# One decode layer, forward and backward: w_o in rows of 8 KB, and zero fills moved to earlier stages

## The chip, the cores and the metric

The kernel runs on one core of a Trainium2 chip. The metric is the time of one execution on the device in microseconds; of several runs the median is taken. A profile is one further execution with the hardware profiler on.

## The reference, cut to what matters

One token passes an adaptive-LayerNorm block: attention of 32 query heads (4 key/value heads, head size 128) over the last 4096 positions of a cache of 65536, then a gated feed-forward network. The program returns the output and, for a given `grad_out`, the gradient of every input.

```python
q = (x @ wq) ...; k, v = k_cache[:, :, Sk - W:, :], v_cache[:, :, Sk - W:, :]   # W = 4096 of Sk = 65536
p = softmax(q k^T * Dh**-0.5);  o = p v;  attn = o.reshape(B, Sq, Hq * Dh) @ wo  # wo: 4096 x 1024
...
mod = (silu(c) @ w_mod).reshape(c.shape[0], 6, 1, -1)          # w_mod: 1024 x 6144
h = layernorm(x) * (1 + ca) + sa;  x = x + ga * A(h)
h = layernorm(x) * (1 + cb) + sb;  x = x + gb * B(h)            # B: (sigmoid(h w_gate) * (h w_up)) w_down, F = 3584
...
_out, _vjp = jax.vjp(_f, A_x, A_k_cache, A_v_cache, A_wq, A_wo, B_w_gate, B_w_up, B_w_down, c, w_mod)
```

With one token almost every gradient of a weight is the outer product of two vectors, as large as the weight. The gradients of the two caches are zero outside the last 4096 positions, so most of what is written is zeros: 120 pieces of about 1 MB, called fills below.

## The kernel before, in words

Everything is laid out by hand in one SBUF buffer, `arena`, of 192 KB in each of 128 partitions; `ar(off, size)` is a slice of it, in KB. The order of instructions on every engine is the order in which the Python code issues them. Five stages follow one another.

1. **Load** (to about 75 us): keys, wq and values are loaded, q, scores and the softmax are made.
2. **N** (75 to 155 us): for each of the 4 key/value heads 32 steps of two matmuls (line 716) on products that VectorE makes (L236). The result `N_sb` holds for every query head a 128x128 matrix. A unit `t_unit(h)` multiplies the stored blocks of wq, `a4[:, j, h, :]`, by that matrix: two matmuls of 128x128 by 512 columns (L674), each evicted at once into the block that it read (L676, or L245 on VectorE). The units of head groups 0 to 2 are put as side jobs at every odd step of this loop; those of group 3 (`tlast`) come at the start of the next stage.
3. **B** (155 to 310 us): 64 chunks (`bch`, L773) of 8 matmuls on TensorE multiply these blocks by w_o. Between them lie the attention output (`attn_units`, L799), the modulation weights, and their transposes.
4. **FFN** (310 to 433 us): seven blocks q of w_up, w_gate and w_down. `front(q)` makes the products with w_up and w_gate on TensorE. `turn(q)` then does the gates; transposes three of eight tiles (`turned`, L1053); multiplies the four rows of w_down on VectorE (`wd_ttr`, L253) and on TensorE (`ffn_mm`, L1073); starts the next load of w_down (`load_wd`, L931, in two halves, from SyncE's queue) as the rows become free; issues fills; and makes the row `dug_b`. Two transposes of side jobs are put between (`side(2)`). VectorE then does the other five tiles and the loads of w_up and w_gate for block q+2 are issued (L942).
5. **End** (433 to 600 us): outer products on VectorE (L249) make the weight gradients, which are stored from there: `dwd` (w_down), `dw_rows` (w_up, w_gate; L1107), `dwo` (w_o; L1247), `sec` (w_mod; L1242), `dwq_tile` (wq; L1290), and the cache gradients (L1286).

**w_o.** `load_wo(u)` (L385) brings 512 rows of w_o into `wo_t[u]`. Before, partition d holds the rows 128 a + d for a = 0..3: one row of 2 KB for each of four heads. The gradient is stored with another order: partition p holds the four rows 4p..4p+3, which are 8 KB in one piece. For it the vector o is put in that order by `op_ps` (L1196, 16 small fp32 matmuls) at the beginning of the End stage.

**Queues.** GpSimd (POOL) issues all fills, most loads and most stores, in the order of the code. SyncE (SP) issues the loads of w_down, a few of w_mod, and some of the last stores.

**Fills.** `zero(n)` issues the next n of the 120 fills. The lists `Z_...` at the top say how many are issued at each place, and `zero(len(zleft))` at the very end issues what is left. A fill can wait for an instruction (`after`), which keeps it from being issued earlier than that. In N and B the pieces are copied from a zeroed piece in DRAM (L203); elsewhere they come from a small tile of zeros (L209; six of them in a narrow form, L194 and L197).

**Buffers of the row gradients.** `dw_rows(k, j, off, ...)` writes a tile of 7 KB a partition at arena offset `off` and stores it. In the End stage three offsets, 16, 32 and 40, go round; VectorE has to wait until the store from a buffer has landed before it writes there again.

Of the kernel before, what the change touches and what calls it, by code (L numbers as in the profile page):

```python
# [10 lines left out]
P = 128  # L11
# [13 lines left out]
HQ = 32  # L25
# [26 lines left out]
Z_KC = [0] * 8  # L52
Z_SM = 4
Z_N = spread(31, 128)
Z_B = [n + (i in (31, 38)) for i, n in enumerate(spread(29, 43))] + [1, 1, 1, 1, 0] + [1, 0, 0, 1, 1, 1, 0, 0] + [1, 0, 1, 0, 1, 0, 0, 0]
Z_FOLD = (1, 1, 1, 2)
Z_FFN = [(1, 0, 1)] + [(1, 1, 1)] * 4 + [(0, 2)]
Z_HAND = (1, 1, 2, 1, 1)
Z_ROWS = (1, 1, 1, 0, 1, 0, 1, 0)
JT = 3  # L60
JV = KD - JT
@with_exitstack
def kernel(
# [314 lines left out]
    def wo_dram(t, u):  # L378
        return t[u * 512:(u + 1) * 512, :].rearrange("(a d) n -> d a n", d=DH)

    def dwo_dram(u):
        return out_5[u * 512:(u + 1) * 512, :].rearrange("(p a) n -> p a n", a=4)

# [263 lines left out]
    def ok_rows():  # L647
        cp(o_col, ok_ps[:, 0:HQ])
        cp(kb_col, ok_ps[:, HQ:2 * HQ])
        cp(o_bf, o_col)  # L650
        lo = scr[:, 768:832].bitcast(FP32)
        for k, (col, rows, s) in enumerate(((o_col, o_rows, 1.0), (kb_col, nkb_rows, -1.0))):
            st = st_cols[k].rearrange("p (a h) -> p a h", a=4)
            cp(st[:, 0, :], col)
            tt(lo, col, st[:, 0, :], ALU.subtract)
            cp(st[:, 3, :], lo)
            cp(st[:, 1, :], st[:, 3 - 3 * k, :])
            cp(st[:, 2, :], st[:, 3 * k, :])
# [46 lines left out]
    for g in range(G):  # L705
        nbank = bank_pair("n_ps", g)
        for t_ in range(KT):
# [35 lines left out]
    tlast = [t_unit(h, "AV") for h in range(HG * 3, HQ)]  # L743


# [38 lines left out]
    for i in range(4):  # L784
        bch()
        tlast[2 * i]()
        tlast[2 * i + 1]()
    bch(2)
# [5 lines left out]
    def attn_units(us, first):  # L794
        for a in range(4):
            for k in range(2):
                for c in range(4):
                    h = 4 * us[c] + a
                    nc.tensor.matmul(attn4[k][32 * c:32 * c + 32, :], lhsT=o_bf[:, h:h + 1].broadcast_to([P, 32]),  # L799
                                     rhs=wo_t[us[c]][:, a, k * 512:(k + 1) * 512], start=(first and a == 0),  # L800
                                     stop=(not first and a == 3), tile_position=(0, 32 * c))
# [245 lines left out]

    def turned(q):
        for j in range(JT):
# [142 lines left out]
    dln2 = vt([P, KD], "dln2")  # L1192
    op_ps = new_acc("op_ps")
    for hh in range(4):
        for a in range(4):
            nc.tensor.matmul(op_ps[32 * hh:32 * hh + 32, 8 * a:8 * a + 8], lhsT=ident_f[:, a::4], rhs=o_col[:, hh::4],  # L1196
                             start=True, stop=True, tile_position=(0, 32 * hh))
    o_perm = kb_col
    cp(o_perm, op_ps[:, 0:HQ])
    mulv(dln2, dh2, cb1)  # L1200
# [26 lines left out]
    dmod_b2 = ar(160, 4)  # L1227
    sec_t = [ar(o, 8) for o in (0, 8, 152, 32, 40, 16, 48, 56)]
    dv_home, dk_home = [ar(o, 32).rearrange("p (g x) -> p g x", g=G) for o in (64, 96)]
# [14 lines left out]
    def dwo(u):  # L1244
        for a in range(4):
            outer_dve(wo_t[u][:, a, :], o_perm[:, 8 * a + u:8 * a + u + 1], dattn_b)
        nc.gpsimd.dma_start(out=dwo_dram(u), in_=wo_t[u])  # L1247

# [96 lines left out]
    bcast(dmod_bf[:, 16:48], 32, dmod_b4, "A")  # L1345
    dw_rows(1, 0, 40, outer_dve)
    zero(Z_ROWS[4])
    dw_rows(1, 1, 16, outer_dve)
    dwo(1)
# [7 lines left out]
    pd = b1k.bitcast(FP32)[:, 0:HQ]  # L1357
    dw_rows(1, 2, 32, outer_dve)
    zero(Z_ROWS[5])
    dw_rows(1, 3, 40, outer_dve)  # L1360
    dcs234 = matvec_T(lambda jb, nb: w2_t[jb][:, nb * P:(nb + 1) * P], dh2_hl, "dcs234")
# [9 lines left out]
    sec(0)  # L1371
    dw_rows(1, 4, 16, outer_dve)
    zero(Z_ROWS[6])
    sec(1)
    dw_rows(1, 5, 32, outer_dve)
    for run in vT_unit[12:]:
        run()
    rebuild_P()
    bcast(dq_bf, HQ, dq_b, "A")
    dw_rows(1, 6, 40, outer_dve)  # L1380
    zero(Z_ROWS[7])
    dw_rows(1, 7, 16, outer_dve)
    sec(2)
# [113 lines left out]
```

## Time and profile before

| | |
|---|---|
| runs | 602.09, 599.39, 599.31 us; median 599.39 |
| the profiled execution | 602.02 us, of which the span from the first to the last instruction is 600.2 us |
| busy in the span | TensorE 415.4 us, VectorE 353.8, ScalarE 247.5, GpSimd 148.0 |
| DMA | 246.54 MB in 33645 packets, mean 411 GB/s |
| HBM | 78.13 MB read, 185.60 MB written |
| fills | 46 from the tile of zeros, 68 from DRAM, 6 in the narrow form |
| loads of w_o | 8 of 1024 KB, median 12.5 us from issue to landing |

The span is counted from the first instruction, and all times below are on that clock. The profiled execution's own time is 1.8 us above its span. The page cuts the span into 40 slices; its row "DMA" tells in tenths how busy the 16 DMA engines were, and the row "GB/s" what they moved. Shares of a queue can add up to over 100%, since packets overlap.

### The profile page before, as it was taken

Reading aid. Unit: us, or ns where it says so; the run is one execution under the profiler, and the core shown is the slowest. Engines: PE = TensorE matmul, PEld = TensorE weight load, DVE = VectorE, ACT = ScalarE, POOL = GpSimd, SP = SyncE. Lnnn points to the kernel's source line nnn. Section 1 sums busy time; section 2 is a strip of 40 time slices with the busy share of each in tenths; the row PEclk is TensorE's granted clock in tenths of the full one; section 3 lists DMA queues with packets and bytes.
Section 4 is the critical chain, followed back from the end, with each engine's and each line's share of the span. In section 5 each row is a group of like instructions: output and inputs, shape, how many; then the busy total and the mean of one; then the engine's idle time right before and its main releaser. Section 6 shows DMA issues by size and latency. Waiting matters only on the chain.

```text
span 600.2 us, 9825 instructions
## 1 busy us (share of the span) xinstructions
PE 415.4 (69%) x4004; PEld 246.7 (41%) x4004; DVE 353.8 (59%) x647; ACT 247.5 (41%) x398; POOL 148.0 (25%) x249
## 2 busy tenths in 40 slices
PE   3996789999999999979776477766652056364300
PEld 2784434334345455435455465555532045131000
DVE  3755499999510030194738488878877056876800
ACT  2489515558211024112246366665632057373200
POOL 3113113212222122222223033241335133241100
PEclk9998699999999999998988578787676557555555
DMA  8999999999999999999999999999999999999997
GB/s 349 421 418 423 411 457 406 430 424 438 433 420 391 453 433 393 461 425 412 387 417 417 347 355 408 409 409 421 424 425 425 429 396 425 423 425 419 419 415 235
DMA packets 33645, 246.54 MB, mean 411 GB/s; under 512 B 4781, under 2 KB 4781, under 8 KB 18864
## 3 DMA queue, kind: packets, MB, share of 16 engines
q0 software_dynamic: 28320, 225.98, 93.8%
q1 hardware_dynamic: 5232, 19.93, 9.5%
q8 instruction: 31, 0.51, 0.3%
q14 instruction: 14, 0.11, 0.1%
q10 hardware_dynamic: 48, 0.01, 0.0%
HBM read 78.13 MB, written 185.60 MB: 439 GB/s over the span
## 4 chain that ended last, share of the span: by engine, by line
PE 37%; DMA 21%; DVE 20%; ACT 8%; issue 7%; POOL 3%; ACTq 0%; POOLq 0%; DVEq 0%; SPq 0%
PE b_ps L773 17%; DMA out_dram<-arena 12%; DVE arena L236 6%; PE n_ps L716 6%; DMA arena<-in_B_w_down_dram 5%; DVE arena L249 4%; DVE arena L253 3%; ACT arena L527 2%; ACT arena L1281 2%; PE t_ps L674 2%; DMA out_dram<-zeros 2%; DVE scr L253 2%; DMA arena<-in_B_w_gate_dram 1%; PE tp_k L506 1%; PE tp_side L916 1%
## 5 line engine op out<-in xcount | busy, mean ns | idle before, releaser
L773 PE MATMUL b_ps<-arena 128*128 128x512 bf16 x512 | 118.6, 384 | 1.1 <-ACT arena L917 1.1
L917 ACT COPY arena<-tp_side 128x1024 bf16<-128x1024 bf16 x62 | 60.8, 1018 | 50.5 <-PE tp_side L916 50.3
L236 DVE TENSOR_TENSOR arena<-arena 128x2048 bf16<-128x2048 bf16 x64 | 76.5, 1223 | 2.3 <-PE n_ps L716 0.3
L773 PEld LDWEIGHTS <-arena 128*128 128x128 bf16 x512 | 49.3, 99 | 58.9 <-issue 5.8
L716 PE MATMUL n_ps<-arena 128*128 128x512 bf16 x256 | 65.6, 378 | 5.8 <-DVE arena L236 4.2
L203 POOL DMA_DIRECT2D out_dram<-out_dram x68 | 33.7, 496 | 116.8 <-PE n_ps L716 38.4
L916 PE MATMUL tp_side<-ident_bf,arena 128*128 128x128 bf16 x496 | 48.2, 262 | 12.7 <-DVE arena L236 4.7
L916 PEld LDWEIGHTS <-arena 128*128 128x128 bf16 x496 | 40.3, 120 | 22.1 <-issue 13.6
L249 DVE TENSOR_SCALAR arena<-arena,h 128x3584 bf16<-128x3584 bf16 (+1 forms) x24 | 28.6, 1192 | 32.1 <-DMA out_dram<-arena 32.1
L209 POOL DMA_DIRECT2D out_dram<-zeros x46 | 25.9, 566 | 67.6 <-DVE rows_all L236 23.0
L716 PEld LDWEIGHTS <-arena 128*128 128x128 bf16 x256 | 24.6, 97 | 41.2 <-issue 15.8
L253 DVE CUSTOM_DVE_ANT_0 arena<-arena,scr 128x1024 bf16<-128x1024 bf16 x35 | 40.8, 1220 | 0.2
L1277 PE MATMUL ps_kv<-arena 32*128 32x512 bf16 x64 | 24.2, 588 | 22.6 <-DVE arena L257 12.8
L253 DVE CUSTOM_DVE_ANT_0 scr<-arena,b1k 128x1024 bf16<-128x1024 bf16 x28 | 34.2, 1223 | 7.5 <-DMA arena<-in_B_w_down_dram 7.0
L1281 ACT ACTIVATE arena<-ps_kv 128x512 bf16<-128x512 f32 x48 | 25.4, 690 | 31.3 <-PE ps_kv L1277 31.1
L676 ACT CAST arena<-t_ps 128x512 bf16<-128x512 f32 x56 | 30.1, 589 | 12.1 <-PE t_ps L674 12.1
L245 DVE CAST arena<-b_ps 128x512 bf16<-128x512 f32 x6 | 4.2, 692 | 50.8 <-PE b_ps L773 50.8
L1053 PE MATMUL tp_ug<-ident_bf,arena 128*128 128x128 bf16 x168 | 14.4, 244 | 17.7 <-ACT arena L1054 17.7
L527 ACT COPY arena<-tp_wq 128x1024 bf16<-128x1024 bf16 x23 | 21.4, 1066 | 7.3 <-PE tp_wq L525 7.3
L1277 PEld LDWEIGHTS <-arena 32*128 32x128 bf16 x64 | 6.9, 117 | 38.7 <-issue 37.8
L1341 PE MATMUL dh_ps<-dattn_bf,arena 128*128 128x1 bf16 x48 | 2.1, 167 | 29.2 <-ACT arena L1337 29.2
L942 POOL DMA_DIRECT2D arena<-in_B_w_up_dram x14 | 10.7, 761 | 43.1 <-DVE dh2acc L253 22.7
(325 smaller groups left out, 686.8 us busy)
## 6 DMA issues: line engine op xcount, KB each, us to landing
out_dram<-zeros POOLq DMA_DIRECT2D x46, 1024.0 KB, 11.8
out_dram<-arena POOLq DMA_DIRECT2D x35, 1024.0 KB, 11.8
out_dram<-arena POOLq DMA_DIRECT2D x16, 896.0 KB, 11.5
arena<-in_A_wq_dram POOLq DMA_DIRECT2D x8, 1024.0 KB, 21.1
arena<-in_A_wo_dram POOLq DMA_DIRECT2D x8, 1024.0 KB, 12.5
arena<-in_w_mod_dram POOLq DMA_DIRECT2D x7, 1024.0 KB, 18.7
arena<-in_B_w_up_dram POOLq DMA_DIRECT2D x14, 512.0 KB, 9.4
arena<-in_B_w_gate_dram POOLq DMA_DIRECT2D x14, 512.0 KB, 13.3
```

Of the source, the lines that this page charges most:

```text
L203: ins = nc.gpsimd.dma_start(out=as_rows(region, BIGP).bitcast(FP32), in_=zero_src[:, 0:P * ZW // 4].rearrange("i (p x) -> (i p) x", p=BIGP ...
L236: return nc.vector.tensor_tensor(out=out, in0=a, in1=b, op=op)
L249: return nc.vector.tensor_scalar(out=out, in0=a, scalar1=s1, scalar2=None, op0=op0)
L253: return nc.vector.tensor_tensor_reduce(out=out, in0=w, in1=b, scale=1.0, scalar=0.0, op0=ALU.mult, op1=ALU.add, accum_out=acc)
L527: nc.scalar.copy(out=blk, in_=tp[:, :])
L676: nc.scalar.copy(out=o, in_=ps)
L716: mm = nc.tensor.matmul(nbank[k][:, :], lhsT=k_nat[:, g, t_ * DH:(t_ + 1) * DH], rhs=vp[:, t_ % 2, 4 * k:4 * k + 4, :].rearrange("p h d -> ...
L773: mm = nc.tensor.matmul(bbank[p][k][:, :], lhsT=a4[:, p, h, :], rhs=wo_t[u][:, a, k * 512:(k + 1) * 512], start=(i == 0 and a == 0), stop= ...
L916: nc.tensor.transpose(tp[:, i * P:(i + 1) * P], blk[:, i * P:(i + 1) * P], ident_bf[:, :])
L917: nc.scalar.copy(out=blk if dst is None else dst, in_=tp[:, :])
L1277: nc.tensor.matmul(ps[:, :], lhsT=rows[r, t8 * P:(t8 + 1) * P], rhs=bd[r, :], start=True, stop=True, tile_position=(32 * tc_, 0))
L1281: nc.scalar.activation(out=o, in_=v, func=ACT.Copy, scale=float(scale))
```

## The change

- **w_o order.** `load_wo` uses the order of the store, `(p a) n -> p a n`: four neighbouring rows, 8 KB, in each partition. What meets w_o has to follow. The T units are rewritten: `t_unit(u, k, a)` takes every fourth column of `N_sb` for four heads and makes four matmuls of 32 output rows each, in the four column tiles of TensorE, into one bank; after a = 3 all four banks are evicted (same number and size of evictions, 64 units of four matmuls instead of 64 matmuls). A fourth bank (`acc`) is used. One unit is put at a side place, 16 a head group instead of 8. o is put in the same order (`shuffle_o`, the code of `op_ps` moved from the End stage to step 6 of the N loop), and the eviction of do puts its columns in that order.
- **turn.** Two of three tiles are transposed first; then the w_down work; the third tile and one side job come after the products `ffn_mm`; the other side job comes after `turned_mm`. The fills of a turn are issued after that side job's instructions.
- **Buffers.** The row gradients use seven offsets: 16, 32, 40 and also 64, 72, 80, 88, where the last four tiles of w_o were.
- **Fills.** One more in `Z_SM` (before the N loop), three more in `Z_N`, two more in `Z_FOLD` (around `front(0)` and `turn(0)`); three fewer in `Z_ROWS` (End). What `zero(len(zleft))` issues at the very end follows from the sum of the lists: 117 of 120 were listed before, 120 are listed now, so three are left over before and none now. Counted in this way six fills leave the End stage.

The diff, cut to its core:

```diff
-Z_SM = 4
-Z_N = spread(31, 128)
+Z_SM = 5
+Z_N = spread(34, 128)
...
-Z_FOLD = (1, 1, 1, 2)
+Z_FOLD = (1, 1, 2, 3)
...
-Z_ROWS = (1, 1, 1, 0, 1, 0, 1, 0)
+Z_ROWS = (1, 1, 0, 0, 0, 0, 0, 0)
...
     def wo_dram(t, u):
-        return t[u * 512:(u + 1) * 512, :].rearrange("(a d) n -> d a n", d=DH)
-
-    def dwo_dram(u):
-        return out_5[u * 512:(u + 1) * 512, :].rearrange("(p a) n -> p a n", a=4)
+        return t[u * 512:(u + 1) * 512, :].rearrange("(p a) n -> p a n", a=4)
...
-        cp(o_bf, o_col)
...
+    o_perm = kb_col
+
+    def shuffle_o():
+        op_ps = new_acc("op_ps")
+        for hh in range(4):
+            for a in range(4):
+                nc.tensor.matmul(op_ps[32 * hh:32 * hh + 32, 8 * a:8 * a + 8], lhsT=ident_f[:, a::4], rhs=o_col[:, hh::4],
+                                 start=True, stop=True, tile_position=(0, 32 * hh))
+        cp(o_perm, op_ps[:, 0:HQ])
+        cp(o_bf, o_perm)
...
-    def t_unit(h, engs="AA"):
+    t_pools = ((psum, "mm"), (pgu, "gu"), (px, "x"), (pacc, "acc"))
+    t_banks = []
+
+    def t_unit(u, k, a, engs="AAAA"):
         def run():
-            for k in range(2):
-                j1 = min(4 * k + 4, NT)
-                ps = new_ps("t_ps").rearrange("p (j m) -> p j m", j=4)[:, 0:j1 - 4 * k, :]
-                o = a4[:, 4 * k:j1, h, :]
-                nc.tensor.matmul(ps, lhsT=N_sb[:, h * P:(h + 1) * P], rhs=o, start=True, stop=True)
-                if engs[k] == "A":
-                    nc.scalar.copy(out=o, in_=ps)
+            pl, tag = t_pools[a]
+            ps = pl.tile([P, 512], FP32, name="t_ps", tag=tag)
+            t_banks.append(ps)
+            for hh in range(4):
+                h = 4 * u + hh
+                nc.tensor.matmul(ps[32 * hh:32 * hh + 32, :].rearrange("p (j m) -> p j m", j=4),
+                                 lhsT=N_sb[:, h * P + a:(h + 1) * P - 3 + a:4], rhs=a4[:, 4 * k:4 * k + 4, h, :],
+                                 start=True, stop=True, tile_position=(0, 32 * hh))
+            if a < 3:
+                return
+            for i in range(4):
+                o, v = a4[:, 4 * k:4 * k + 4, 4 * u + i, :], t_banks[i].rearrange("p (j m) -> p j m", j=4)
+                if engs[i] == "A":
+                    nc.scalar.copy(out=o, in_=v)
                 else:
-                    cp(o, ps)
+                    cp(o, v)
+            t_banks.clear()
         return run
...
+            elif s == 6:
+                shuffle_o()
...
-            jobs.extend(t_unit(h, "AA") for h in range(HG * g, HG * g + HG))
+            jobs.extend(t_units(g))
...
     def turn(q, fills=0):
         gates()
-        turned(q)
-        side(2)
+        turned(q, range(JT - 1))
         wd_ttr(0)
         hh_ops(q)
         first = wd_ttr(1)
         ffn_mm(q, 0)
         if q + 1 < NB:
             load_wd(q + 1, 0, 2)
+        ffn_mm(q, 2)
+        turned(q, (JT - 1,))
+        side(1)
         zero(fills, wd_ttr(2, 3))
-        ffn_mm(q, 2)
         if q + 1 < NB:
             load_wd(q + 1, 2, 2)
         last = dug_part(q)
         turned_mm(q)
+        side(1)
         return first, last
...
-        nc.scalar.copy(out=do_sb, in_=do4[:, :])
+        nc.scalar.copy(out=do_sb.rearrange("q (h r a) -> q a h r", h=4, a=4),
+                       in_=do4.rearrange("q (a h r) -> q a h r", a=4, h=4))
...
-    dw_rows(0, 5, 40, outer_dve)
-    dw_rows(0, 6, 16, outer_dve)
+    dw_rows(0, 5, 64, outer_dve)
+    dw_rows(0, 6, 72, outer_dve)
     zero(Z_ROWS[3])
-    dw_rows(0, 7, 32, outer_dve)
+    dw_rows(0, 7, 80, outer_dve)
...
-    dw_rows(1, 0, 40, outer_dve)
+    dw_rows(1, 0, 88, outer_dve)
...
```

The later calls of `dw_rows` and the list `sec_t` take their offsets in the new round; `attn_units` reads o in the new order, `dwo` stores through `wo_dram`.

More of the change, by code (lines that the diff above doesn't have):

```diff
@@ L666, in build_bd, with t_units @@
                                  scale=sel[:, HG * g + i:HG * g + i + 1])
-    def t_unit(h, engs="AA"):
+    t_pools = ((psum, "mm"), (pgu, "gu"), (px, "x"), (pacc, "acc"))
+    t_banks = []
+    def t_unit(u, k, a, engs="AAAA"):
         def run():
-            for k in range(2):
-                j1 = min(4 * k + 4, NT)
-                ps = new_ps("t_ps").rearrange("p (j m) -> p j m", j=4)[:, 0:j1 - 4 * k, :]
-                o = a4[:, 4 * k:j1, h, :]
-                nc.tensor.matmul(ps, lhsT=N_sb[:, h * P:(h + 1) * P], rhs=o, start=True, stop=True)
-                if engs[k] == "A":
-                    nc.scalar.copy(out=o, in_=ps)
-                else:
-                    cp(o, ps)
-        return run
+            pl, tag = t_pools[a]
[12 more added lines that the diff above has]
+                    nc.scalar.copy(out=o, in_=v)
+                else:
+                    cp(o, v)
+            t_banks.clear()
+        return run
+    def t_units(g, engs="AAAA"):
+        return [t_unit(u, k, a, engs) for u in (2 * g, 2 * g + 1) for k in range(2) for a in range(4)]
     jobs.clear()
@@ L739 @@
         if g < 3:
-            jobs.extend(t_unit(h, "AA") for h in range(HG * g, HG * g + HG))
+            jobs.extend(t_units(g))
     load_wo(3)
     side(len(jobs))
-    tlast = [t_unit(h, "AV") for h in range(HG * 3, HQ)]
+    tlast = t_units(3, "AVAV")
     bq = []
@@ L785 @@
         bch()
-        tlast[2 * i]()
-        tlast[2 * i + 1]()
+        for run in tlast[4 * i:4 * i + 4]:
+            run()
     bch(2)
@@ L797, in attn_units @@
                 for c in range(4):
-                    h = 4 * us[c] + a
-                    nc.tensor.matmul(attn4[k][32 * c:32 * c + 32, :], lhsT=o_bf[:, h:h + 1].broadcast_to([P, 32]),
+                    n = 8 * a + us[c]
+                    nc.tensor.matmul(attn4[k][32 * c:32 * c + 32, :], lhsT=o_bf[:, n:n + 1].broadcast_to([P, 32]),
                                      rhs=wo_t[us[c]][:, a, k * 512:(k + 1) * 512], start=(first and a == 0),
@@ L1046, in ug_flat, with turned @@
         return ug_v[:, q % 2, j // 4, j % 4, :, :].rearrange("p k f -> p (k f)")
-    def turned(q):
-        for j in range(JT):
+    def turned(q, js=range(JT)):
+        for j in js:
             w, tp = ug_flat(q, j), new_tp("tp_ug")
@@ L1192 @@
     dln2 = vt([P, KD], "dln2")
[L1193 to L1199, printed above, removed]
     mulv(dln2, dh2, cb1)
@@ L1227 @@
     dmod_b2 = ar(160, 4)
-    sec_t = [ar(o, 8) for o in (0, 8, 152, 32, 40, 16, 48, 56)]
+    sec_t = [ar(o, 8) for o in (0, 8, 152, 16, 32, 40, 48, 56)]
     dv_home, dk_home = [ar(o, 32).rearrange("p (g x) -> p g x", g=G) for o in (64, 96)]
@@ L1246, in dwo @@
             outer_dve(wo_t[u][:, a, :], o_perm[:, 8 * a + u:8 * a + u + 1], dattn_b)
-        nc.gpsimd.dma_start(out=dwo_dram(u), in_=wo_t[u])
+        nc.gpsimd.dma_start(out=wo_dram(out_5, u), in_=wo_t[u])
     def rebuild_P():
@@ L1345 @@
     bcast(dmod_bf[:, 16:48], 32, dmod_b4, "A")
-    dw_rows(1, 0, 40, outer_dve)
+    dw_rows(1, 0, 88, outer_dve)
     zero(Z_ROWS[4])
-    dw_rows(1, 1, 16, outer_dve)
+    dw_rows(1, 1, 40, outer_dve)
     dwo(1)
@@ L1357 @@
     pd = b1k.bitcast(FP32)[:, 0:HQ]
-    dw_rows(1, 2, 32, outer_dve)
+    dw_rows(1, 2, 16, outer_dve)
     zero(Z_ROWS[5])
-    dw_rows(1, 3, 40, outer_dve)
+    dw_rows(1, 3, 32, outer_dve)
     dcs234 = matvec_T(lambda jb, nb: w2_t[jb][:, nb * P:(nb + 1) * P], dh2_hl, "dcs234")
@@ L1371 @@
     sec(0)
-    dw_rows(1, 4, 16, outer_dve)
+    dw_rows(1, 4, 40, outer_dve)
     zero(Z_ROWS[6])
     sec(1)
-    dw_rows(1, 5, 32, outer_dve)
+    dw_rows(1, 5, 16, outer_dve)
     for run in vT_unit[12:]:
@@ L1379 @@
     bcast(dq_bf, HQ, dq_b, "A")
-    dw_rows(1, 6, 40, outer_dve)
+    dw_rows(1, 6, 32, outer_dve)
     zero(Z_ROWS[7])
-    dw_rows(1, 7, 16, outer_dve)
+    dw_rows(1, 7, 40, outer_dve)
     sec(2)
```

## The prediction

> **What bounds the kernel now.** I read the page's slices first, then busy time by stage, then who waited in the stages where the transfers dip, then single issues in the timeline. The slices show transfers without a break:
>
> ```profile
> DMA  8999999999999999999999999999999999999997
> GB/s 349 421 418 423 411 457 406 430 424 438 433 420 391 453 433 393 461 425 412 387 417 417 347 355 408 409 409 421 424 425 425 429 396 425 423 425 419 419 415 235
> ```
>
> No compute engine is above 69% (PE 415.4 us). So the time is the bytes (246.54 MB) at the rate of a full stretch, 411 to 430 GB/s, plus the time in which no transfer was waiting. Moving a fill saves nothing in itself; it pays where it fills a hole. Slices 22 and 23 (347, 355) are a hole, and by stage (columns: window, length, busy time and count of PE, PEld, DVE, ACT, POOL, then clock, DMA share, GB/s):
>
> ```profile
> 310.00:335.00 25.00, 16.77 (x256) 13.05 (x256) 15.86 (x34) 16.89 (x23) 5.17 (x8) 0.81 1.07 402
> 335.00:350.00 15.00, 8.82 (x144) 6.80 (x144) 10.98 (x24) 4.49 (x5) 2.71 (x5) 0.64 0.90 303
> 350.00:433.00 83.00, 56.73 (x836) 46.76 (x835) 71.96 (x153) 54.11 (x71) 24.69 (x40) 0.74 1.12 411
> 433.00:485.00 52.00, 15.47 (x230) 11.19 (x230) 26.00 (x68) 11.95 (x14) 15.48 (x22) 0.63 1.05 426
> 485.00:490.00 5.00, 4.23 (x69) 4.15 (x70) 1.72 (x2) 3.39 (x7) 1.23 (x2) 0.50 0.86 358
> 490.00:569.00 79.00, 41.03 (x363) 20.97 (x361) 60.68 (x109) 37.38 (x69) 21.10 (x32) 0.54 1.02 421
> ```
>
> Two holes: 335 to 350 lacks (411 - 303) x 15 us = 1.62 MB, 3.9 us of full rate; 485 to 490 lacks (424 - 358) x 5 = 0.33 MB, 0.8 us. The first one's cause, from the waits in 312 to 350 (total, times, longest):
>
> ```profile
> POOL out_dram L209 <- DVE rows_all L236: 11.6, 1, 11.6
> ...
> DVE scr L253 <- DMA arena<-in_B_w_down_dram: 7.0, 2, 4.9
> ```
>
> GpSimd issues nothing from 329.8 to 341.35: its next fill waits for the last w_down row of turn(1), and that half of w_down, issued at 319.94, is there only at 338.5. The second one's cause, from the waits of VectorE in 430 to 570:
>
> ```profile
> DVE arena L249 <- DMA out_dram<-arena: 38.4, 11, 13.9
> ```
>
> The outer products wait 38.4 us for stores from their own buffers (13.9 of it at 475.6, for offset 16), and the queue runs dry at 488.
>
> **The change part by part.** One fill is 1.049 MB; in the trace fills land 2.41 to 2.45 us apart.
>
> *Four fills earlier in softmax and N.* No hole lies there (80 us at 432 GB/s), so they only push what is queued behind them back by 4 x 2.43 = 9.7 us. GpSimd issues at most eight transfers ahead (in B each lands 19 us after issue, 8 x 2.42), the rest of the push is blocked issue. Who waits: w_o(3), landing at 174.1 and used at about 175.7, so chunk 10 of B comes some 8 us late; the ga weights (landed 210.77, used at 210.72); the last modulation load (landed 305.84, its product starts 306.23). B is gated by such loads anyway, so FFN starts about 9.7 us later, with the same transfers queued behind it as before: no transfer time is lost, and TensorE gains 9.7 us of cover up to there.
>
> *T in column tiles.* 256 matmuls for 64. The price is shown by the attention products, 128x32 by 512 in four column tiles:
>
> ```profile
> L799 PE MATMUL attn<-arena,o_bf x64: 379/379/390, 179.2 to 191.3; 128*32 128x512 bf16 x64
> ```
>
> The chain of waits has 32 of them in 1.84 us, 0.23 for four, against 1.73/8 = 0.216 for one full matmul. 64 x 0.014 = +0.9 us, and up to 64 x 0.3 more if four weight loads (97 ns each) don't hide. With one unit at each of 48 side places, where 0.43 us were taken at each of 24, the N loop (VectorE's 1.23 of 1.29 us a pair of steps) keeps its pace. shuffle_o adds its 1.47 us of PE there. Under the 9.7 us cover: 0; beyond it each us costs one only once the eight transfers ahead are used up.
>
> *w_o in 8 KB rows.* The eight loads land 2.53 to 2.70 us after the transfer before them (one 3.95, with other traffic), about 2.55; the wq loads, 8 KB rows, 2.48 apart. 8 x 0.07 = 0.5 us less. Bounds: 0, and 0.8 by packets (4096 B 171 ns, 8192 B 329 ns). I take 0.5. The Trainium skill, page "DMA: Bandwidth & Descriptors", section Specifications, puts line rate at transfers of 512 B and over; by that this term is 0 and the sum below 0.5 us smaller. The landings speak mildly against it.
>
> *turn.* ffn_mm(0, 0) at 318.50 no longer waits for the third tile and two side jobs (its input is there at 315.9); the first half of w_down can be asked for up to 1.5 us earlier, when wd_ttr(1) ends (317.3). The second half, which ends the hole, still waits for wd_ttr(3) (319.9): 0 taken, up to 1.5 gained. On TensorE and ScalarE the third tile and a side job (0.61 + 1.01 us each) now come after w_down's second half, while VectorE does two rows (2.5 us): they end about when dug_part can start. Fills were already queued behind wd_ttr(3).
>
> *Two fills around turn(0).* They bring 2.10 MB, 4.9 us, into a hole of 3.9. But w_down shares the engines with them. With some 16 us queued, SP's load issued at 319.07 had moved nothing by 325.3 (first view: 319.1 to 325.3, second: 325.3 to 336):
>
> ```profile
> q0 software_dynamic: 397, 2.63, 114.3%
> ```
> ```profile
> q0 software_dynamic: 589, 3.39, 83.9%
> q1 hardware_dynamic: 287, 1.05, 26.4%
> ```
>
> The one issued at 336.57, with 7 us queued, starts at 337.5: (6.4 - 1.0) / (16 - 7) = 0.6 us of delay per us queued. Seven transfers were ahead at 318.15, so the limit of eight lets one more in: 2.4 x 0.6 = 1.5 us later. Recovered 4.9 - 1.5 = 3.4 us; bounds 0 (next part) and 3.9. The Trainium skill, same page, section "Queues, rings and completion order", says that an engine takes turns between queues packet by packet; by that SP's load would not start later for what GpSimd has queued, and all 3.9 would come back, 0.5 more in the sum. The 6.4 us before the first packet do not look like it.
>
> *Seven buffers.* Offsets 64 to 88 hold w_o tiles whose stores landed at 468.6 to 478.0; the row tiles that waited until 475.6, 480.2 and 487.3 get them 5 to 9 us sooner (471.0, 473.4, 478.0). The hole at 485 goes: 0.7 of 0.8.
>
> *Six fills out of the End stage, op_ps out of its start.* 14.6 us fewer transfers there, after a start that is 9.7 + 4.9 - 3.4 = 11.2 us later. VectorE has 38.4 us of store waits to absorb that. If it absorbs nothing, the last products end at 569 + 11.2 = 580.2; the transfers would end at 595.9 - 4.6 = 591.3, and the last four stores (4 x 2.44 = 9.8 us) just fit. So nothing is added. op_ps (1.56 us of VectorE's waiting at 434.6) is worth 0 while transfers bound, 1.5 otherwise.
>
> Sum: 3.4 + 0.7 + 0.5 = 4.6 us less. On the profiled execution: span 600.2 to 595.6, own time 602.0 to 597.4. The median of the runs lies 2.6 below that execution's time; 599.4 - 4.6 = **594.8 us**.
>
> **The rivals.**
>
> *The hole moves instead of closing* (0.20). w_down goes back by as much as the two fills bring: 4.9 x 0.6 = 2.9 us of start if both count, and packets shared with 8 KB fills for the rest. For it: 18.5 us for w_down's landing with a full queue, 7.4 with a short one. Against: the limit of eight. Then 0.5 + 0.7 + 0.5 = 1.7: 597.7 us.
>
> *The End stage starves* (0.13), the one that ends slower. The three fills that left its middle (464, 489, 501) were what the queue lived on while VectorE waited. If GpSimd's limit of eight, and not the buffers, holds VectorE's stores up, the waits stay, and each missing fill leaves its own length: +7.3, against -(3.4 + 0.5): 602.8. It decides once the time from issue to landing falls under one fill's 2.4 us between 464 and 535. The shortest there now is 4.9 us (488.77), and the buffers should raise it, so I hold it unlikely.
>
> *T in column tiles does not overlap* (0.04). 256 x 0.216 = 55 us instead of 13.8: +41, less the cover of 9.7: about 630. The attention products speak against it.
>
> That the fills do not leave as named is possible in part: I count six, not seven; the sum uses six.
>
> **How the numbers follow.** Forecast 0.63, rivals 0.20, 0.13, 0.04. About 0.5%, 3.0 us, is what can be told from no change. Of the forecast 0.58 lies under 596.4; the moved hole is mostly within 0.5% (0.16), and partly recovered faster (0.03); starvation is slower but for 0.03 within. Faster 0.61, same 0.24, slower 0.15. Best case 3.9 + 0.8 + 0.8 and 1.5 from w_down's earlier half: 7.0, 592.4; a little under it for the runs' own spread, 591.5. The upper end takes in the moved hole with nothing recovered and part of the starved case: 600.5. The forecast's own range is 592.4 to 597.
>
> **What would show it.** Right: 335 to 350 (some 10 us later) at over 390 GB/s; no slice under 390 between the first and the last; FFN's start near 320; the last GpSimd issue is a cache store, with no fill behind it; VectorE's store waits in the End stage under 30 us; w_o landings 2.5 us apart; TensorE's T units at some 0.23 us for four matmuls. Wrong: a new dip in GB/s at any place, above all in 460 to 540; w_down landing more than 20 us after its issue; N ending much after 157. A time above 597 with all slices full would mean the rate, not the holes, has changed.

## The result, and the profile after

The changed kernel takes 595.80 us (median of 5 runs, 594.98 to 596.39). The kernel before, timed on the same chip in the same job, takes 599.31 to 602.09 us (median of 5 runs 601.58). The ratio is 0.9915, with a 95% interval of 0.9891 to 0.994: faster by 0.9%. The forecast was 594.8 us. The profiled execution took 596.39 us, as much as the slowest of the five runs; its span is 594.6 us (before: 602.02 and 600.2). Over all jobs the runs of the kernel before lie in two groups, about 599.0 to 600.0 and about 601.4 to 602.2 us, and the execution that was profiled belongs to the upper one; this matters below.

The page's slices of the changed kernel:

```profile
DMA  8999999999999999999999999999999999999997
GB/s 351 422 418 421 423 464 392 425 425 428 424 409 458 419 438 429 414 404 451 413 408 399 418 409 408 400 411 409 424 382 428 423 429 421 425 408 413 409 413 321
```

The two low slices in the middle (347, 355) are gone, there is a new shallow one (382, at 431 to 446 us), and the last slice is fuller (321 against 235). The new one breaks the prediction's sign that no slice between the first and the last would be under 390. The same stages as before the prediction, in the changed kernel (window, length, busy time and count of PE, PEld, DVE, ACT, POOL, then clock, DMA share, GB/s):

```profile
310.00:335.00 25.00, 18.43 (x244) 13.19 (x243) 12.46 (x28) 12.03 (x17) 7.51 (x12) 0.81 1.07 417
335.00:350.00 15.00, 8.55 (x127) 6.39 (x126) 10.39 (x23) 7.78 (x11) 4.13 (x6) 0.73 1.20 418
350.00:433.00 83.00, 58.80 (x870) 47.51 (x869) 66.45 (x139) 49.83 (x66) 23.29 (x36) 0.69 1.13 410
433.00:485.00 52.00, 25.11 (x257) 18.15 (x254) 38.07 (x92) 20.00 (x21) 16.24 (x25) 0.60 1.04 415
485.00:490.00 5.00, 1.50 (x32) 1.17 (x32) 1.40 (x2) 4.45 (x5) 0.53 (x1) 0.50 1.01 427
490.00:569.00 79.00, 43.77 (x420) 24.30 (x421) 57.40 (x104) 39.31 (x73) 18.98 (x29) 0.54 1.01 415
```

335 to 350 went from 303 to 418 GB/s and 485 to 490 from 358 to 427, as forecast. FFN starts later now (`front(0)` at 322.49 us, before at 311.68), so what stood in 335 to 350 stands in about 345 to 360; there it is 407 GB/s. 433 to 485 and 490 to 569 lost 11 and 6 GB/s, and 319 to 323, just before `front(0)`, has 351 (before 420). The waits of VectorE and GpSimd in 312 to 350 (total, times, longest):

```profile
POOL out_dram L209 <- DVE rows_all L236: 7.0, 1, 7.0
...
DVE scr L253 <- DMA arena<-in_B_w_down_dram: 3.6, 2, 2.6
```

The wait for w_down is 3.6 us instead of 7.0, GpSimd's longest is 7.0 instead of 11.6. VectorE's waits in 430 to 570 for stores from its own buffers:

```profile
DVE arena L249 <- DMA out_dram<-arena: 31.3, 11, 6.6
```

The longest fell from 13.9 to 6.6 us.

One thing the prediction had not looked at. The transfers at the end, in windows of 2 us, first before and then after:

```profile
592.00:594.00 2.00, 0.00 (x0) 0.00 (x0) 0.00 (x0) 0.00 (x0) 0.00 (x0) 0.50 1.17 307
594.00:596.00 2.00, 0.00 (x0) 0.00 (x0) 0.00 (x0) 0.00 (x0) 0.00 (x0) 0.50 0.11 29
596.00:598.00 2.00, 0.00 (x0) 0.00 (x0) 0.00 (x0) 0.00 (x0) 0.00 (x0) 0.50 0.00 0
598.00:600.00 2.00, 0.00 (x0) 0.00 (x0) 0.00 (x0) 0.00 (x0) 0.00 (x0) 0.50 0.00 0
```
```profile
590.00:592.00 2.00, 0.00 (x0) 0.00 (x0) 0.00 (x0) 0.00 (x0) 0.00 (x0) 0.50 0.52 217
592.00:594.00 2.00, 0.00 (x0) 0.00 (x0) 0.00 (x0) 0.00 (x0) 0.00 (x0) 0.50 0.04 16
```

Before, the last packet ends at 595.4 us and the span runs on to 600.2: 4.8 us in which nothing moves. After, the last packet ends at 592.9 and the span at 594.6: 1.7 us. So of the 5.6 us by which the profiled span is shorter, 3.1 us lie behind the last packet, and only 2.5 us in the transfers. The last issues tell the two kernels apart; first before, then after, from the timeline:

```profile
567.99 1.99 SPq L1286 DMA_DIRECT2D out_dram<-arena  x2
568.46 1.06 POOL L1286 DMA_DIRECT2D out_dram<-arena  x2 [16.45 <-issue]
569.50 1.59 POOL L209 DMA_DIRECT2D out_dram<-zeros  x3
```
```profile
573.06 2.03 SPq L1304 DMA_DIRECT2D out_dram<-arena  x2
573.53 1.06 POOL L1304 DMA_DIRECT2D out_dram<-arena  x2 [16.60 <-issue]
```

Before, three fills of GpSimd stand last. The last of them lands at 595.93, SyncE has drained at 596.26, and GpSimd takes its part in the end of the program only at 599.50: until 599.45 the trace has it in one instruction, a DRAIN. After, GpSimd's last store lands at 587.69 and SyncE's at 593.34. GpSimd's DRAIN ends at 590.85, also some 3 us after its last landing, but a store of SyncE is still under way then; SyncE has drained at 593.84 and GpSimd follows at 593.88. This "tail" is the theory that the second half of the experiments tests.

### The profile page after: what moved, and what is told of

The parts are those of the page before. It is cut to its first block, busy times and chain, and to the rows that moved or that the text cites. A ratio compares the mean times of both kernels' runs of the same rounds, so it can differ in the third digit from the quotient of the medians.

```text
span 594.6 us, 10189 instructions
## 1 busy us (share of the span) xinstructions
PE 429.0 (72%) x4167; PEld 247.9 (42%) x4196; DVE 354.8 (60%) x647; ACT 248.3 (42%) x398; POOL 143.5 (24%) x249
## 4 chain that ended last, share of the span: by engine, by line
PE 35%; DMA 30%; DVE 14%; issue 10%; ACT 5%; POOL 1%; ACTq 0%; POOLq 0%; DVEq 0%
DMA out_dram<-arena 13%; PE b_ps L796 12%; PE n_ps L737 9%; DMA out_dram<-out_dram 6%; DMA arena<-in_B_w_gate_dram 5%; PE t_ps L685 4%; DVE arena L253 3%; DMA out_dram<-zeros 3%; DMA arena<-in_B_w_up_dram 3%; DVE scr L253 2%; DVE arena L249 2%; ACT arena L524 2%; DVE arena L236 2%; PE tp_k L503 1%; PE w_ps L466 1%
## 5 line engine op out<-in xcount | busy, mean ns | idle before, releaser
L796 PE MATMUL b_ps<-arena 128*128 128x512 bf16 x493 | 116.2, 384 | 2.6 <-ACT arena L940 1.1
L236 DVE TENSOR_TENSOR arena<-arena 128x2048 bf16<-128x2048 bf16 x64 | 77.7, 1224 | 8.9 <-PE n_ps L737 5.3
L203 POOL DMA_DIRECT2D out_dram<-out_dram x72 | 35.7, 497 | 127.5 <-PE n_ps L737 56.2
L939 PE MATMUL tp_side<-ident_bf,arena 128*128 128x128 bf16 x496 | 52.7, 278 | 8.8 <-DVE arena L236 5.4
L693 ACT CAST arena<-t_ps 128x512 bf16<-128x512 f32 x56 | 28.9, 598 | 39.9 <-PE t_ps L685 39.9
L209 POOL DMA_DIRECT2D out_dram<-zeros x42 | 23.2, 555 | 58.3 <-DVE rows_all L236 24.9
L685 PE MATMUL t_ps<-arena 128*32 128x512 bf16 x256 | 24.1, 399 | 3.4 <-ACT arena L760 2.8
L1077 ACT COPY arena<-tp_ug 128x1024 bf16<-128x1024 bf16 x21 | 20.5, 1008 | 7.7 <-PE tp_ug L1076 7.7
```

Source lines behind the costliest of these rows:

```text
L203: ins = nc.gpsimd.dma_start(out=as_rows(region, BIGP).bitcast(FP32), in_=zero_src[:, 0:P * ZW // 4].rearrange("i (p x) -> (i p) x", p=BIGP ...
L236: return nc.vector.tensor_tensor(out=out, in0=a, in1=b, op=op)
L685: nc.tensor.matmul(ps[32 * hh:32 * hh + 32, :].rearrange("p (j m) -> p j m", j=4), lhsT=N_sb[:, h * P + a:(h + 1) * P - 3 + a:4], rhs=a4[: ...
L693: nc.scalar.copy(out=o, in_=v)
L796: mm = nc.tensor.matmul(bbank[p][k][:, :], lhsT=a4[:, p, h, :], rhs=wo_t[u][:, a, k * 512:(k + 1) * 512], start=(i == 0 and a == 0), stop= ...
L939: nc.tensor.transpose(tp[:, i * P:(i + 1) * P], blk[:, i * P:(i + 1) * P], ident_bf[:, :])
```

## The experiments

Ratios are against the kernel before on the same chip, with 95% intervals. "Tail" is the time from the last packet to the end of the span.

**All moved fills back.** The changed kernel with the lists of before.

```diff
-Z_SM = 5
-Z_N = spread(34, 128)
+Z_SM = 4
+Z_N = spread(31, 128)
...
-Z_FOLD = (1, 1, 2, 3)
+Z_FOLD = (1, 1, 1, 2)
...
-Z_ROWS = (1, 1, 0, 0, 0, 0, 0, 0)
+Z_ROWS = (1, 1, 1, 0, 1, 0, 1, 0)
```

> The changed kernel with the four fill lists of before (Z_SM 4, Z_N 31, Z_FOLD 1 1 1 2, Z_ROWS 1 1 1 0 1 0 1 0); w_o rows, turn and seven buffers stay. Theory 'holes' (the time is the bytes at full rate plus the time in which no transfer waits; the moved fills pay because two of them lie in the hole at the start of FFN): that hole comes back, 3 to 4 us, so the span is 597.5 to 598.5 against 594.6, and the stretch 335 to 350 (or its place some us later) moves some 300 GB/s. Rival 'work' (the gain is from the w_o rows, the turn or the buffers; fills only change the order): within 0.7 us of the changed kernel, 594 to 595.3.

Measured: 604.38 us, ratio 1.0063 (1.0045 to 1.0082), tail 4.6 us. A miss in size: without the moved fills the rest of the change makes the kernel slower than before. Two holes open, and three fills stand last again:

```profile
75.00:110.00 35.00, 30.64 (x181) 12.20 (x179) 30.81 (x41) 6.17 (x17) 7.96 (x15) 0.95 1.06 409
315.00:335.00 20.00, 13.21 (x212) 10.27 (x209) 11.11 (x25) 10.35 (x16) 3.70 (x7) 0.84 1.02 364
335.00:365.00 30.00, 22.95 (x347) 18.14 (x348) 25.85 (x55) 20.16 (x28) 10.12 (x15) 0.73 1.07 384
```

The first line is the N loop, where the changed kernel has 422 GB/s: (422 - 409) x 35 us = 0.46 MB, 1.1 us. The other two make 376 over 50 us, where the changed kernel has 396 and 412, together 406: 1.5 MB, 3.6 us. With 2.9 us of tail that is 7.6 us; the spans differ by 8.0 and the medians by 8.6. (Five other kernels with the changed kernel's code up to 110 us have 434 to 441 in the first window, so 422 is at the low end.)

**The moved fills alone.** The kernel before with the four lists of the change: the diff above read upwards.

> The kernel before with only the four fill lists of the change. Theory 'holes': the hole at 335 closes (-3.4 us), FFN starts some 10 us later; with three buffers VectorE keeps its long waits for stores, and the three fills that the queue lived on in 464 to 501 are gone, so the hole at 485 grows by one to three fills (2.4 to 7.3 us): span 599 to 604. Rival 'fills are all' (buffers, w_o and turn add nothing): 596.8, with the hole at 485 no larger than the 0.8 us of before.

Measured: 596.76 us, 0.9939 (0.9921 to 0.9957), tail 1.7 us. Most of the gain is there with nothing but lists edited. The expectation had a hole of one to three fills open without the new buffers (span 599 to 604); the span is 595.0. The queue only thins out at 480 to 520 (404 GB/s against 425 after, (425 - 404) x 40 us = 0.84 MB, 2.0 us), which the tail outweighs.

**w_o back.** The changed kernel with the old order of w_o, the old T units and the old places of `op_ps` and of the do eviction.

```diff
-        return t[u * 512:(u + 1) * 512, :].rearrange("(p a) n -> p a n", a=4)
+        return t[u * 512:(u + 1) * 512, :].rearrange("(a d) n -> d a n", d=DH)
...
-    tlast = t_units(3, "AVAV")
+    tlast = [t_unit(h, "AV") for h in range(HG * 3, HQ)]
```

> The changed kernel with the w_o order, the T units, shuffle_o and the eviction of do of before; fills, turn and buffers as changed. Theory 'holes': the N loop ends some 10 us sooner (155 instead of 165), which buys nothing, since FFN is gated by loads behind the fills; w_o's eight loads cost 0.6 to 0.8 us more; the new dip at 95 to 100 of the changed kernel (338 GB/s, 1.0 us), which came when the N loop's start was held up by shuffle_o, goes away. Span 594 to 595, within 0.7 us of the changed kernel. Rival 'work': N's 10 us come through, 588 or less; or w_o's rows are the gain, 597 or more.

Measured: 595.27 us, 0.9914 (0.9897 to 0.9932). The N loop is some 10 us shorter, and the first product at FFN's start (`g_ps`, of the modulation) is at 316.6 us, in the changed kernel at 316.9: the loads queued ahead of it decide, not N. The dip at 95 to 100 us has 327 GB/s here and 262 in the changed kernel (not 338, as the expectation has it). The w_o part is worth nothing measurable here.

**Three buffers.** The changed kernel with offsets 16, 32 and 40 only.

```diff
-    dw_rows(0, 5, 64, outer_dve)
+    dw_rows(0, 5, 40, outer_dve)
```

(and ten more calls like it, and the old order of `sec_t`)

> The changed kernel with the three offsets 16, 32, 40 of before for the row gradients and the order of sec_t of before. Theory 'holes', as in the slower rival of the prediction (the End stage starves): VectorE's waits for stores stay at 24 us between 465 and 500, the queue lacks three fills there, a hole of one to three fills opens: span 597.5 to 602. Rival (the buffers are not needed; fewer transfers shorten the waits by themselves): 594.6 to 595.4.

Measured: 596.44 us, 0.9935 (0.9917 to 0.9954). VectorE's longest store wait is 12.5 us again, the sum of these waits 32.4, and 480 to 520 has 412 GB/s: 13 x 40 us = 0.52 MB, 1.2 us. The medians differ by 0.6 us, inside the overlap of the intervals. The End stage does not starve.

**The early fills back.** The changed kernel with the lists of softmax and N as before; the four fills go to the End stage.

```diff
-Z_SM = 5
-Z_N = spread(34, 128)
+Z_SM = 4
+Z_N = spread(31, 128)
...
-Z_ROWS = (1, 1, 0, 0, 0, 0, 0, 0)
+Z_ROWS = (1, 1, 2, 0, 1, 0, 1, 0)
```

> The changed kernel with Z_SM and Z_N as before (four fills fewer before and in the N loop); these four go to places 2, 4 and 6 of Z_ROWS, none is left for the very end. By the prediction these four fills lie in no hole and cost or gain nothing: 594 to 595.3. By the theory that came out of the first experiment (the N loop is held up at its start by shuffle_o and by slower T units, so its fills come late and the queue runs dry there) the dips at 85 to 100 and 185 open, 2 to 3 us: 596.5 to 597.8.

Measured: 598.04 us, 0.9958 (0.994 to 0.9976); 2.2 us above the changed kernel. From the windows of the kernel before, the changed kernel and this one:

```profile
75.00:110.00 35.00, 30.95 (x144) 13.13 (x143) 34.11 (x42) 14.89 (x36) 9.21 (x17) 1.00 1.10 435
```
```profile
75.00:110.00 35.00, 30.39 (x176) 12.27 (x178) 30.69 (x40) 6.29 (x17) 8.74 (x17) 0.95 1.07 422
```
```profile
75.00:110.00 35.00, 30.95 (x176) 12.20 (x174) 30.17 (x39) 6.03 (x16) 7.82 (x15) 0.90 1.03 398
```

(422 - 398) x 35 us = 0.84 MB, 2.0 us. So the four fills do not lie beside a full queue: with the new T units and `shuffle_o` the N loop issues its fills later, the queue runs dry (215 GB/s in 95 to 100, before 416), and the four fills pay for that. All kernels together say the same of this window: 431 to 439 GB/s in the six with the old N loop, with the early fills (fills alone 437) or without them (before 435); 398 and 409 with the new N loop and without the early fills; 422 to 441 with both.

**The two fills around turn(0) back.** They go to the End stage, not to its end.

```diff
-Z_FOLD = (1, 1, 2, 3)
+Z_FOLD = (1, 1, 1, 2)
...
-Z_ROWS = (1, 1, 0, 0, 0, 0, 0, 0)
+Z_ROWS = (1, 1, 1, 0, 1, 0, 0, 0)
```

> The changed kernel with Z_FOLD as before (two fills fewer around turn(0)); these two are issued at places 2 and 4 of Z_ROWS in the End stage, so that no fill is left for the very end. Theory 'holes': the hole at the start of FFN comes back whole (the kernel before lacked 1.8 MB in 335 to 365), 4 to 4.7 us: span 598.5 to 599.5 against 594.6. Rival (w_down, not the fills, sets that stretch; the hole only moved): within 1.5 us, 594 to 596.

Measured: 593.99 us, 0.9891 (0.9871 to 0.9911). The prediction's main term was 3.4 us for these two fills; taken back, the kernel is not slower, by the medians 1.8 us faster (the intervals overlap). VectorE's wait for w_down in 312 to 350 is down to 0.4 us (3.6 in the changed kernel), and there is no hole:

```profile
335.00:365.00 30.00, 22.15 (x344) 17.67 (x342) 25.68 (x53) 20.13 (x27) 8.79 (x13) 0.78 1.11 401
```

**turn back.** The changed kernel with the old order in `turn`.

```diff
-        turned(q, range(JT - 1))
+        turned(q)
+        side(2)
...
-        ffn_mm(q, 2)
-        turned(q, (JT - 1,))
-        side(1)
```

> The changed kernel with the turn of before (three tiles and two side jobs ahead of the w_down products). Theory 'holes': the order of turn moves no transfer by more than 1.5 us and the queue has some 10 us in it there: span 594.3 to 595.6. Rival (the earlier w_down products are part of the gain): w_down's loads come some 1.5 us later in each of seven turns, VectorE waits, 597 or more.

Measured: 595.58 us, 0.992 (0.9899 to 0.9941). VectorE waits 6.0 us for w_down in 310 to 360, in the changed kernel 3.6; in the time the order in `turn` is worth nothing that can be seen.

**No fill at the very end.** The kernel before, with the three fills that were left over put among the row gradients.

```diff
-Z_ROWS = (1, 1, 1, 0, 1, 0, 1, 0)
+Z_ROWS = (1, 1, 2, 1, 2, 0, 1, 0)
```

> The kernel before with one edit: the three fills that were left for the very end are issued earlier in the End stage (Z_ROWS 1 1 2 1 2 0 1 0); nothing is moved to N or FFN. Theory 'tail' (seen by comparing the two traces: GpSimd is ready for the end only 3.5 us after the landing of its last transfer, 3.2 us after SyncE; with a fill last this is in the span, with a SyncE store last it is hidden): the end comes 3 us sooner after the last transfer, and the hole at 485 (0.8 us) is filled: span 596 to 597.2, the hole at 335 stays. Rival (what is moved within one stage changes nothing): 599.5 to 600.5.

Measured: 595.03 us, 0.9915 (0.9894 to 0.9936), tail 1.7 us. This one line gives the ratio of the whole change. The transfers gain too: 480 to 520 has 424 GB/s against 414 before (0.4 MB, 1.0 us). And the code up to 463 us is that of before, yet the hole is not the same. Windows of before and of this kernel:

```profile
335.00:365.00 30.00, 19.86 (x312) 15.70 (x312) 23.99 (x51) 14.24 (x18) 8.54 (x13) 0.71 1.00 351
```
```profile
335.00:365.00 30.00, 20.26 (x328) 15.93 (x324) 26.39 (x55) 18.02 (x25) 10.05 (x15) 0.83 1.08 383
```

The wait for w_down is 3.0 us here, 7.0 there. (383 - 351) x 30 us = 0.96 MB, 2.3 us. So a good half of the 1.8 MB that this window lacked before was a matter of the one execution that was profiled. The 2.3 us are about what lies between the two groups of runs of before; that this hole is what separates the groups is not shown, since only one execution of the kernel before has a profile.

**GpSimd last.** The changed kernel with the last two stores of the key gradient on GpSimd's queue instead of SyncE's.

```diff
-        kv_store(out_2, dk_home, g, nc.gpsimd if g < 2 else tail)
+        kv_store(out_2, dk_home, g, nc.gpsimd)
```

> The changed kernel with one edit: all four stores of the key gradient are issued by GpSimd, instead of two by GpSimd and two by SyncE, so that GpSimd's transfer lands last, as it does before the change. Same bytes, no fill moved. Theory 'tail' (GpSimd is ready for the end only 3.5 us after its last landing): span 597 to 598.2 against 594.6, with 4.7 us between the last packet and the end of the span instead of 1.7. Rival (the end depends on the last transfer, whoever issued it): 594 to 595.3.

Measured: 598.89 us, 0.9988 (0.998 to 0.9997). The last packet ends at 592.0 us, no later than in the changed kernel, and the span is 596.5:

```profile
590.00:592.00 2.00, 0.00 (x0) 0.00 (x0) 0.00 (x0) 0.00 (x0) 0.00 (x0) 0.50 0.30 127
592.00:594.00 2.00, 0.00 (x0) 0.00 (x0) 0.00 (x0) 0.00 (x0) 0.00 (x0) 0.50 0.00 0
```

Which queue has the last transfer is worth 3 us (598.89 against 595.80; tail 4.5 against 1.7) with two stores moved and nothing else. SyncE has drained at 592.87, GpSimd's last store landed at 592.50, and GpSimd, again in a DRAIN until then, follows only at 595.79.

**The two fills around turn(0) alone.** The kernel before with the main term of the prediction, and nothing else; the three fills at the very end stay.

```diff
-Z_FOLD = (1, 1, 1, 2)
+Z_FOLD = (1, 1, 2, 3)
...
-Z_ROWS = (1, 1, 1, 0, 1, 0, 1, 0)
+Z_ROWS = (1, 1, 1, 0, 0, 0, 0, 0)
```

> The kernel before with one edit: two fills go from places 4 and 6 of Z_ROWS to Z_FOLD (1 1 2 3), around turn(0); three fills stay for the very end. This is the main term of the prediction by itself: 3.4 us less, 596.8, if closing the hole at 335 pays. By the theory after the second experiments (the profiled execution showed the hole larger than most executions have it; the same code had one of 2.0 us in another execution, and two fills less in the End stage open the hole at 485 further): 0 to 1.5 us less, 598.5 to 600.

Measured: 602.20 us, 1.0041 (1.0026 to 1.0055). Slower by 0.4% where the sum gave 3.4 us less and the later theory 0 to 1.5 us less: both missed. (All runs lie at 600.9 to 602.9 us, where the upper group of before is; the 0.4% comes from the lower group.) The two fills are transferred, and w_down comes later for it; the window, and VectorE's wait in 312 to 350:

```profile
335.00:365.00 30.00, 17.84 (x273) 14.71 (x274) 21.58 (x45) 13.11 (x17) 7.01 (x11) 0.67 1.04 364
```
```profile
DVE scr L253 <- DMA arena<-in_B_w_down_dram: 9.0, 2, 7.0
```

How much later is seen in the load of the second half of w_down, from issue to landing, in the chains of the kernel before and of this one:

```profile
319.94 18.48 DMA arena<-in_B_w_down_dram
```
```profile
321.19 20.97 DMA arena<-in_B_w_down_dram
```

When SyncE issues w_down's first half, eight transfers of GpSimd are under way, seven before: one more got in, as the prediction said, and the second half takes 2.5 us more. The hole is still there, and the End stage, with two fills fewer, has 402 GB/s in 480 to 520 (414 before): 0.48 MB, 1.1 us lost. So this run prices the two fills together with what they leave behind in a kernel with three buffers.

**A version from these results.** The changed kernel without the two fills around turn(0); one of them goes to the end of FFN, against the dip at 430 to 440 us, one to the End stage.

```diff
-Z_FOLD = (1, 1, 2, 3)
-Z_FFN = [(1, 0, 1)] + [(1, 1, 1)] * 4 + [(0, 2)]
+Z_FOLD = (1, 1, 1, 2)
+Z_FFN = [(1, 0, 1)] + [(1, 1, 1)] * 4 + [(0, 3)]
...
-Z_ROWS = (1, 1, 0, 0, 0, 0, 0, 0)
+Z_ROWS = (1, 1, 1, 0, 0, 0, 0, 0)
```

> The changed kernel with Z_FOLD as before (1 1 1 2), one of these two fills put at the last place of Z_FFN (0, 3), where the queue of the changed kernel runs thin at 430 to 440, the other at place 2 of Z_ROWS. Theory 'holes and tail': as the run with Z_FOLD back (593.99 us, span 592.1), and the dip at 430 to 440 (0.9 us without transfers, some 1.2 us of bytes) closes: span 590.8 to 591.6, 592.5 to 593.3 us. Rival (that dip is only moved): 593.5 to 594.5.

Measured: 594.02 us, 0.9904 (0.989 to 0.9919). The dip closes (420 to 445: 423 GB/s, in the changed kernel 401), and the time is that of the kernel that only took the two fills back (593.99): nothing more is gained.

**The same with the old w_o part** (the diff of "w_o back" on top of this one).

> The run before this one with the w_o order, T units, shuffle_o and eviction of do of the kernel before. Tells what the w_o part is worth once the queue holds. Theory: w_o's rows of 8 KB save 0.6 to 0.8 us of transfer, T's slower units cost nothing: this kernel is 0.6 to 0.8 us slower than the one with the new order, 593.2 to 594. Rival (what the transfers win is lost where FFN's work sets the pace, as in the first experiments): the same within 0.3 us, or faster.

Measured: 594.42 us, 0.9914 (0.99 to 0.9927). The w_o part is worth 0.4 us by the medians, with overlapping intervals.

The fastest kernels are these three, 593.99, 594.02 and 594.42 us; by the medians all are below the changed kernel's 595.80.

## Why the prediction was right, and where it was not

The time was right to 1.0 us, the sign too, and most of what was to show it was seen: 418 GB/s in 335 to 350, FFN's start at 316.9 us (`front(0)` at 322.5), a cache store as GpSimd's last issue, a longest store wait of 6.6 us (the sum, 31.3, was to be under 30), w_o landing 2.45 us apart in the median. One sign failed: a slice between the first and the last is under 390 (382). But the sum of 4.6 us was made of other things than the chip's gain, and that the time came so near is in part luck. The span was forecast at 595.6 us and is 594.6: it fell by 1.0 us more than the sum. The median was then put 2.6 us below the profiled execution, as it was before the change; it lies 0.6 below. The two errors go against each other, and the median is 1.0 us above its forecast. The 2.6 us did not carry over: they take the forecast to the lower group of runs of before, while the hole was priced from an execution of the upper one.

- **The hole at 335 us (3.4 us): the step that failed.** "The limit of eight lets one more in: 1.5 us later" put w_down's delay too low. The one more got in, and the second half of w_down took 2.5 us longer from issue to landing (20.97 against 18.48); in the changed kernel it takes 15.5 us, and 11.8 with the two fills taken back. For that the rival "the hole moves" had 2.9 us, and it describes the term by itself better: it made the kernel 0.4% slower, with 1.1 us lost in the End stage among that. In the changed kernel the fills do hold the rate up (406 GB/s over 315 to 365, without them 399; 0.31 MB, 0.8 us), but removing them cost nothing in the end. The size was wrong before that: a good half of the hole was missing in another execution of the same code.
- **"Beside a full queue" (0 us) for the four early fills: wrong, and in the change's favour only together with its other half.** The new T units and `shuffle_o` stretch the N loop: groups of 19.9 us before take 21.0 to 22.7 us, and the last load of w_o is issued at 166.8 instead of 155.8 us. Fills in N are issued in step with the loop, so it thins the queue; the four fills put back what it took, 2.0 us. The prediction took "the N loop keeps its pace" and "no hole lies there" from the kernel before, where both were true. Its sign of trouble, "N ending much after 157", was seen.
- **T (0.23 us for four): mis-sized.** The timeline of the changed kernel in the N loop:

```profile
139.92 0.41 PE L685 MATMUL t_ps<-arena 128*32 128x512 bf16 x4
140.27 0.82 PE L737 MATMUL n_ps<-arena 128*128 128x512 bf16 x3
141.24 0.41 PE L685 MATMUL t_ps<-arena 128*32 128x512 bf16 x4
141.58 1.04 PE L737 MATMUL n_ps<-arena 128*128 128x512 bf16 x4
...
168.35 1.06 PE L685 MATMUL t_ps<-arena 128*32 128x512 bf16 x16 [0.37 <-ACT arena L760]
```

  The four do run together (they start within 10 ns of one another and last 0.41 us), but the next full matmul starts 0.35 us after the first of them, not 0.23. The last line is from the stage after N, where four groups follow one another in 1.06 us, so (1.06 - 0.41) / 3 = 0.22 us apart: the price that was read from the attention products holds for groups in a row, as those are, and not for one group between full matmuls. At 48 places that is 48 x 0.12 = 5.8 us more of TensorE than forecast; here TensorE has no gap left. `shuffle_o` took more than its 1.47 us, too: the first group of N, which has no T units, ends 3.7 us later (its last products start at 98.72 us, before at 94.99), and VectorE waits 2.1 us for `op_ps` there. The rival "does not overlap" would have shown 0.86 us for four; it fell. That N's lateness costs nothing while the fills keep the queue full held (w_o back: 595.27).
- **The end (0 us): the largest thing that was left out.** The prediction counted three fills fewer at the very end as transfers, and took the 4.3 us behind the last landing as given. They became 1.3 us. Against that, its transfers were to end at 591.3 and ended (last landing) at 593.3: 2.0 us of the terms above did not come. That is how the span came out 1.0 us shorter than forecast: 3.0 us that were not in the sum, less 2.0 us of it that did not come.
- **w_o rows (0.5 us).** The landings went from about 2.55 to 2.45 us, 8 x 0.1 = 0.8 us of transfer, at the upper bound. In the time it is 0.4 us or nothing. The Trainium skill, page "DMA: Bandwidth & Descriptors", section Specifications, puts line rate at 512 B and over; the landings differ from that by 4%, the time could not tell.
- **The hole at 485 (0.7 us): right.** 427 GB/s; over 480 to 520 it is 425, with three buffers 412, 1.2 us less. But the three fills from the very end close it as well (424), without the buffers.
- **turn (0): right. Starvation: did not come**, not even with three buffers, where the queue only thinned (412, in "the moved fills alone" 404).

Not settled: why the runs of before fall into two groups (they do on each of the three chips that the experiments ran on), why the versions without the two fills are 1.4 to 1.8 us below the changed kernel (the intervals overlap), and why 520 to 570 us runs at 410 to 415 GB/s in some kernels and 418 to 421 in others. What GpSimd's DRAIN does in its last 3.2 to 3.5 us the trace does not show; that it follows GpSimd's own last transfer is seen in all 14 profiles, and that it costs time only where this transfer ends last is shown by one edit in each direction (no fill at the very end, GpSimd last).

## What to carry to other kernels

Where transfers bind, look also at what comes behind the last packet, and at which queue issued the last transfer: here one edited list gave what the whole change gave. A fill, or any work put in a hole, pays only while the queue is dry and nothing urgent stands behind it; ask what in the same change makes the queue dry, since two parts can only cancel. And before a hole is priced from one profiled execution, compare that execution's own time with the runs: it was 2.6 us above the median, and another execution of the same code had 2.3 us less of the hole.

## What the runs showed of the hardware

- **The last transfer's queue.** In all 14 kernels with a profile, the tail is 4.5 to 4.8 us where a transfer of GpSimd ends last (four kernels) and 1.6 to 1.7 us where one of SyncE does (ten). In all 14 GpSimd's closing DRAIN ends 3.2 to 3.5 us after the landing of its own last transfer. Where that is the last one, GpSimd is ready 3.3 us (595.79 against 592.50) to 3.6 us (599.50 against 595.93) after it; SyncE, where its own is the last, 0.5 us after (593.84 against 593.34). The Trainium skill, page "DMA: Bandwidth & Descriptors", section "Anatomy of one DMA — SWDGE (gpsimd) path", gives a fixed part of about 2 us to each such transfer, most of it the wait for the last byte's receipt. The 3.3 us here come after the landing that the trace records, on top of that.
- **Executions of one code differ in one place.** The hole at 335 us had 351 GB/s and a wait of 7.0 us for w_down in one execution, 383 and 3.0 in another with the same code up to there.
- **GpSimd's transfers under way.** In none of the 14 profiles are more than eight transfers that GpSimd issued under way at once, and in all of them eight are reached.
- **A packed group of four matmuls** (128x32 by 512) lasts 0.41 us; the start of the next such group follows 0.22 us after its own start, that of a full matmul 0.35 us after it.
